# Hedgehog attention with spectral mixing: the last Z and Y copied whole and split by small transfers

## The chip, the cores and the metric

The kernel runs on one core of a Trainium2 chip. The metric is device time in microseconds for one execution. The engines are PE (TensorE, matrix products), DVE (VectorE), ACT (ScalarE), POOL (GpSimd) and SP (SyncE, which only issues transfers). PE writes its results into PSUM; DVE and ACT bring them from there to SBUF; transfers (DMA) move data between SBUF and DRAM, and between places in SBUF.

## What is computed

Linear attention with exponential features over 8 batches, 8 heads, 576 tokens and head width 64 gives x of 8 x 576 x 512. A spectral layer follows: of the Fourier transform of x along the tokens the lowest 64 modes are multiplied by complex 512 x 512 weights, one pair for each mode, and transformed back. A pointwise layer with ReLU ends it.

```python
def _moe_ref(x, w_r, w_i, w_ch):
    X = np.fft.rfft(x, axis=1)
    Y = np.zeros_like(X)
    Xr, Xi = (np.real(X[:, :n_modes]), np.imag(X[:, :n_modes]))
    Yr = np.einsum('bmd,mde->bme', Xr, w_r) - np.einsum('bmd,mde->bme', Xi, w_i)
    Yi = np.einsum('bmd,mde->bme', Xr, w_i) + np.einsum('bmd,mde->bme', Xi, w_r)
    Y[:, :n_modes] = Yr + 1j * Yi
    y = np.fft.irfft(Y, n=S, axis=1)
    u = x + y
    return (u + np.maximum(u @ w_ch, 0.0)).astype(np.float32)
```

The weights w_r and w_i are 2 x 64 x 512 x 512 numbers of 4 bytes and make up most of what is read.

## The kernel before

Everything up to the result of the last modes is the same in both kernels. In a first loop (L549) the attention is worked out in 32 pieces and x is written to `xs_all` in bf16, 5 chunks of 128 tokens for each batch (the fifth is half full). Beside it the weights stream in through POOL's queue (`weights`, L156), and `mode_mm` (L390) multiplies them as they land, in 32 steps (`groups`, L108; most of them are 8 modes for one of four groups of 128 input features). The second loop (L727 to L756) does the last ten of these steps and, between them, multiplies x by w_ch (`times_w`, result `xw`).

In the last group of features the sums are finished: `mode_sum` (L439) gives `yst`, 8 modes by 4 kinds of row, transposed on PE into `ptY` (L742) and copied to `sY` (L745). After two such steps 16 modes are complete, and `by_batch` (L691) is called with P = 0 to 3. It forms, with rows sorted by batch, Z = Y times w_ch in `psZ` (PSUM buffer T0, L699) and Y itself in `psR` (T1, L705). A batch number is j + 4 h, and in PSUM j is the block of 32 partitions and h the half of the columns. The four `copy(j)` then move block j to partitions 32 P to 32 P + 31 of `zall` and `yall`, where all modes of a batch lie one below the other: Z by ACT (L712), Y by DVE (L713). For P < 3 these copies are spread over later steps. For P = 3 the list holds five pieces: products and copy for half h = 0 and j = 0, the same for h = 1, then both halves of j = 1, 2 and 3, the last of them all on ACT.

What is left is the transform back and the sum, over 20 units (L799 to L831). A unit is two chunks of 128 tokens of one batch, or (a half unit) the fifth chunks of two batches. Batches come in pairs b and b + 4. With b = 0 to 3 a pair has four full units and one half unit: units 0 to 4, 5 to 9, 10 to 14, and 15 to 19 (in the last pair the half unit comes first). For each unit, in PE's order:

- `add_xw` (L771): an identity product brings xw into `psB`; `add_z` (L778) adds the inverse transform of Z from `zall`; ACT takes the ReLU of it to the output tile `o` (L780).
- `spec` (L787, L790): an identity product brings x into `psA`, the inverse transform of Y from `yall` is added, and DVE adds psA to o (L793). In ten "late" units (`late`, L675) the identity product is left out, and POOL adds x to o instead (L797).

`psB` and `psA` lie in PSUM buffers T2 and T3, or T0 and T1, two banks each. T0 and T1 hold psZ and psR until the last copies are done, so units 0 to 3 all use T2 and T3, and from unit 4 on even units use T2/T3 and odd ones T0/T1. Between units 0 to 3 the five pieces of `copies` are placed.

Instructions of one engine run in the order in which they are written (`manual_schedule`). SP issues the output transfers (L831), two of 256 KB for each full unit and two of 128 KB for each half unit, in its own fixed order: those of a late unit two units after it, the others at once. The output tiles `of` of a batch pair share three buffers, so pair 3 writes where pair 0 was.

Of the kernel before, what the change touches and what calls it, by code (L numbers as in the profile page):

```python
# [20 lines left out]
DMODEL = 512  # L21
# [5 lines left out]
def kernel(  # L27
# [128 lines left out]
    def weights(k):  # L156
        g, gi = groups[k]
        wt = {}
        for ri, w in ((0, moe_w_r), (1, moe_w_i)):
            t = pw.tile([128, 8, DMODEL], BF16, name=f"w{'ri'[ri]}", tag=f"w{ri}")  # L160
            if gi >= 0:
                nc.gpsimd.dma_start(  # L162
                    t, w[8 * gi:8 * gi + 8, g * 128:(g + 1) * 128, :].rearrange("m p e -> p m e"))
            else:
                for x in range(2):
                    mx = 16 * (-1 - gi) + 8 * x
                    nc.gpsimd.dma_start(
                        t[64 * x:64 * x + 64],
                        w[mx:mx + 8, g * 64:(g + 1) * 64, :].rearrange("m p e -> p m e"))
            wt[ri] = t  # L170
        W[k] = wt
# [252 lines left out]
    def mode_sum(k, psY, pb=None):  # L424
        g, gi = groups[k]
        if gi < 0:
            G = -1 - gi
            if g == 0:
                nc.vector.tensor_copy(Yacc[:, 2 * G:2 * G + 2, :], psY)
            else:  # L430
                nc.vector.tensor_tensor(
                    out=Yacc[:, 2 * G:2 * G + 2, :], in0=psY, in1=Yacc[:, 2 * G:2 * G + 2, :],
                    op=ALU.add)
        elif g < 3:
            nc.vector.tensor_tensor(  # L435
                out=Yacc[:, gi, :], in0=psY, in1=Yacc[:, gi, :], op=ALU.add)
# [254 lines left out]
    def by_batch(sY, P):  # L691
        cols = [sY[:, dc].rearrange("p g c -> p (g c)") for dc in range(4)]
        psZ = psum.tile([128, 2, DMODEL], F32, name="psZ", tag="T0")
        psR = psum.tile([128, 2, DMODEL], F32, name="psR", tag="T1")

        def mm_z(h):
            for dc in range(4):
                for j in range(4):
                    nc.tensor.matmul(psZ[32 * j:32 * j + 32, h, :], lhsT=cols[dc][:, j + 4 * h::8],  # L699
                                     rhs=wchb[:, dc, :], start=(dc == 0), stop=(dc == 3))  # L700

        def mm_r(h):
            for dc in range(4):
                for j in range(4):
                    nc.tensor.matmul(  # L705
                        psR[32 * j:32 * j + 32, h, dc * 128:(dc + 1) * 128],
                        lhsT=cols[dc][:, j + 4 * h::8], rhs=ident_b, start=True, stop=True)

        def copy(j, h=None, one=False):
            r = slice(32 * j, 32 * j + 32)  # L710
            bs, hs = (slice(j, None, 4), slice(0, 2)) if h is None else (j + 4 * h, h)
            nc.scalar.copy(zall[32 * P:32 * P + 32, bs, :], psZ[r, hs, :])  # L712
            (nc.scalar.copy if one else nc.vector.tensor_copy)(  # L713
                yall[32 * P:32 * P + 32, bs, :], psR[r, hs, :])

        if P < 3:
            for f in (mm_z, mm_r):
                for h in range(2):
                    f(h)
            copies.extend([lambda j=j: copy(j) for j in range(4)])  # L720
        else:

            copies.extend([lambda: (mm_z(0), mm_r(0), copy(0, 0)),
                           lambda: (mm_z(1), mm_r(1), copy(0, 1)),
                           lambda: copy(1), lambda: copy(2), lambda: copy(3, None, True)])

    with tc.manual_schedule():  # L727
        plan = {22: 3, 23: 3, 24: 2, 25: 2, 26: 2, 27: 1, 28: 2, 29: 1, 30: 1, 31: 0}
        while k_out < 32:
            k = k_out  # L730
            gi = groups[k][1]
            while k_in < min(k_out + NW, 32):
                weights(k_in)
                k_in += 1
            yst = mode_sum(k, mode_mm(k, "T3"), pb)
            k_out += 1
            if yst is not None:
                if ahead:
                    times_w()
                pt = psum.tile([128, 4, 128], BF16, name="ptY", tag="T3")  # L740
                for dc in range(4):
                    nc.tensor.transpose(pt[:, dc, :], yst[:, dc * 128:(dc + 1) * 128], ident_b)  # L742
                if gi % 2 == 0:
                    sY = pb.tile([128, 4, 2, 128], BF16, name="sY", tag="sY")
                nc.vector.tensor_copy(sY[:, :, gi % 2, :], pt)  # L745
                if gi % 2 == 1:
                    by_batch(sY, gi // 2)
            pieces(plan[k])
            if k <= 24 or k % 2 == 0:
                assert not copies  # L750
                for tag in ("T0", "T1"):
                    if reorder:
                        reordered(tag)
            if k == 30:
                times_w()
        assert not todo and not ahead and not reorder and len(copies) == 5  # L756

# [21 lines left out]
                             start=False, stop=True)  # L779
        nc.scalar.activation(u["o"], ps[:, 0, :] if u["half"] else ps, ACT.Relu)  # L780

    def spec(u):
        ps = psum.tile([128, 2, DMODEL], F32, name="psA", tag=u["tags"][1])
        late = u["late"]
        if not late:
            for r, x, b, c, idn, ci in parts(u):
                nc.tensor.matmul(ps[r, x, :], lhsT=idn, rhs=xs_all[:, b * NCH + c, :],  # L787
                                 start=True, stop=False)
        for r, x, b, c, idn, ci in parts(u):
            nc.tensor.matmul(ps[r, x, :], lhsT=ci, rhs=yall[:, b, :],  # L790
                             start=late, stop=True)
        o = u["o"]
        nc.vector.tensor_tensor(out=o, in0=ps[:, 0, :] if u["half"] else ps, in1=o, op=ALU.add)  # L793
        if late:
            b, c = u["bc"][0]
            i = b * NCH + c
            nc.gpsimd.tensor_tensor(out=o, in0=o, in1=xs_all[:, i:i + 2, :], op=ALU.add)  # L797

    units = []  # L799
    for b in range(4):  # L800
        of = [pw.tile([128, 4, DMODEL], F32, name="of", tag=f"w{x}") for x in range(2)]
        o4 = Yacc[:, 2 * b, :]
        us = []
        for x in range(2):
            out_v = out[b + 4 * x].rearrange("(p n) e -> p n e", n=9)
            for c in (0, 2):
                us.append(dict(bc=((b + 4 * x, c), (b + 4 * x, c + 1)), o=of[x][:, c:c + 2, :],
                               late=(x, c) in late[b], half=False,
                               dmas=[(out_v[:, 5 * jj + c:5 * jj + c + 2, :],
                                      of[x][jj::2, c:c + 2, :]) for jj in range(2)]))  # L810
        u4 = dict(bc=((b, 4), (b + 4, 4)), o=o4, late=False, half=True,
                  dmas=[(out[b + 4 * x].rearrange("(p n) e -> p n e", n=9)[:, 4, :],
                         o4[64 * x:64 * x + 64]) for x in range(2)])
        units += [u4] + us if b == 3 else us + [u4]

    with tc.manual_schedule():
        LAG = 2
        copies.pop(0)()
        for n in range(len(units) + LAG):
            if n < len(units):  # L820
                u = units[n]
                u["tags"] = ("T2", "T3") if n % 2 == 0 or n < 4 else ("T0", "T1")
                add_xw(u)
                add_z(u)
                spec(u)
                if copies:
                    copies.pop(0)()
            for lag, is_late in ((LAG, True), (0, False)):
                if 0 <= n - lag < len(units) and units[n - lag]["late"] == is_late:
                    for dst, src in units[n - lag]["dmas"]:  # L830
                        nc.sync.dma_start(dst, src)  # L831

# [29 lines left out]
```

## Time and profile before

| | us |
|---|---|
| time, median of 3 runs | 461.41 (459.97 to 462.96) |
| profiled execution, its time | 459.81 |
| profiled execution, its span | 458.0 |
| busy in the span: PE, DVE, ACT, POOL | 302.9, 299.2, 263.7, 195.2 |
| mean granted clock of PE | 0.885 |

The page gives shares over the whole span. The chain that ended last names the weights' transfers with 19% (w_i) and 7% (w_r), and the queue that carries them is busy all the time:

```profile
q0 software_dynamic: 75600, 76.49, 100.6%
q1 hardware_dynamic: 8576, 20.06, 12.6%
```

The columns are the queue, its packets, its megabytes and the time its packets took as a share of 16 engines' span. The second line is SP's queue with the inputs v and the outputs. Of the 40 slices of the span, the last four or so are the 20 units:

```profile
PE   3465687755587677646464665676678878867893
DVE  6588889867988788866656473766332274464774
ACT  4575787843676868755545453755333445663762
POOL 4956567445563346634344332533021113000593
DMA  6999999999999999999999999999999999991488
```

Each digit is one slice of 11.45 us, in tenths busy. The weights' stream ends in the slice in which DMA falls to 1; the outputs fill the last two.

### The profile page before, as it was taken

Reading aid. Unit: us, or ns where it says so; the run is one execution under the profiler, and the core shown is the slowest. Engines: PE = TensorE matmul, PEld = TensorE weight load, DVE = VectorE, ACT = ScalarE, POOL = GpSimd, SP = SyncE. Lnnn points to the kernel's source line nnn. Section 1 sums busy time; section 2 is a strip of 40 time slices with the busy share of each in tenths; the row PEclk is TensorE's granted clock in tenths of the full one; section 3 lists DMA queues with packets and bytes.
Section 4 is the critical chain, followed back from the end, with each engine's and each line's share of the span. In section 5 each row is a group of like instructions: output and inputs, shape, how many; then the busy total and the mean of one; then the engine's idle time right before and its main releaser. Section 6 shows DMA issues by size and latency. Waiting matters only on the chain.

```text
span 458.0 us, 11074 instructions
## 1 busy us (share of the span) xinstructions
PE 302.9 (66%) x4637; PEld 196.9 (43%) x4637; DVE 299.2 (65%) x418; ACT 263.7 (58%) x531; POOL 195.2 (43%) x246
## 2 busy tenths in 40 slices
PE   3465687755587677646464665676678878867893
PEld 2354465543454545534343443343344544433341
DVE  6588889867988788866656473766332274464774
ACT  4575787843676868755545453755333445663762
POOL 4956567445563346634344332533021113000593
PEclk9987999975976979997769685988999999999998
DMA  6999999999999999999999999999999999991488
GB/s 181 193 230 216 213 210 218 229 207 229 218 218 218 229 218 229 219 228 217 219 207 221 216 219 218 207 209 206 207 207 207 207 207 207 207 173 50 170 317 292
DMA packets 84385, 97.31 MB, mean 212 GB/s; under 512 B 3312, under 2 KB 77168, under 8 KB 84336
## 3 DMA queue, kind: packets, MB, share of 16 engines
q0 software_dynamic: 75600, 76.49, 100.6%
q1 hardware_dynamic: 8576, 20.06, 12.6%
q8 instruction: 36, 0.59, 0.5%
q14 instruction: 13, 0.11, 0.1%
q10 hardware_dynamic: 160, 0.07, 0.1%
HBM read 163.64 MB, written 9.44 MB: 378 GB/s over the span
## 4 chain that ended last, share of the span: by engine, by line
DMA 30%; DVE 23%; issue 21%; PE 10%; POOL 7%; ACT 7%; SPq 1%; DVEq 0%; ACTq 0%; POOLq 0%
DMA wi<-in_moe_w_i_dram 19%; DVE mkq L233 7%; DMA wr<-in_moe_w_r_dram 7%; DMA q<-in_q_dram 4%; DVE xs_all L336 4%; DVE nd L322 3%; DVE tB L315 3%; ACT AA L240 3%; POOL vaug L270 2%; ACT e L262 2%; DVE of L793 2%; PE psNB L305 2%; PE psB L771 1%; PE psB L778 1%; PE psA L790 1%
## 5 line engine op out<-in xcount | busy, mean ns | idle before, releaser
L270 POOL TENSOR_TENSOR vaug<-vn,ee 128x576 bf16<-128x576 f32 x64 | 72.7, 1156 | 59.5 <-ACT ee L255 53.6
L240 ACT ACTIVATE AA<-psT 128x1024 bf16<-128x1024 f32 x64 | 62.0, 1021 | 42.3 <-PE psT L208 41.8
L162 POOL DMA_DIRECT2D wr<-in_moe_w_r_dram x24 | 21.9, 911 | 115.9 <-PE psY L416 109.5
L262 ACT ACTIVATE e<-mkq 64x4 f32<-64x4 f32 (+1 forms) x128 | 26.3, 206 | 66.3 <-DVE mkq L233 64.0
L244 ACT ACTIVATE AA<-psk 128x1024 bf16<-128x1024 f32 x64 | 61.3, 1009 | 0.0
L416 PE MATMUL psY<-wi,XT 128*32 128x512 bf16 x192 | 24.1, 448 | 29.1 <-DMA wi<-in_moe_w_i_dram 29.1
L416 PEld LDWEIGHTS <-XT 128*32 128x32 bf16 x384 | 17.7, 167 | 55.9 <-issue 47.9
L233 DVE TENSOR_REDUCE mkq<-psk 128x8 f32<-128x1024 f32 x32 | 38.8, 1212 | 0.8 <-PE psk L199 0.7
L233 DVE TENSOR_REDUCE mkq<-psq 128x8 f32<-128x1024 f32 x32 | 38.9, 1217 | 0.3
L435 DVE TENSOR_TENSOR Yacc<-psY,Yacc 128x512 f32<-128x512 f32 x16 | 11.0, 689 | 42.6 <-PE psY L416 42.5
L797 POOL TENSOR_TENSOR of<-of,xs_all 128x1024 f32<-128x1024 f32 x10 | 21.1, 2130 | 41.5 <-DVE of L793 41.5
L661 ACT CAST xw<-psW 128x1024 bf16<-128x1024 f32 x17 | 17.2, 1012 | 36.5 <-PE psW L659 36.5
L286 PE MATMUL kvz<-vaug,AA 64*128 64x65 bf16 x1152 | 29.5, 211 | 9.7 <-POOL vaug L275 8.0
L190 DVE COPY kT<-ptr 128x640 bf16<-128x640 bf16 x32 | 15.7, 491 | 30.5 <-PE ptr L184 30.5
L416 PE MATMUL psY<-wr,XT 128*32 128x512 bf16 x192 | 24.2, 458 | 16.0 <-DMA wr<-in_moe_w_r_dram 7.3
L315 DVE TENSOR_TENSOR tB<-psNB,e 128x650 f32<-128x650 f32 x32 | 26.6, 833 | 11.4 <-PE psNB L305 10.8
L659 PE MATMUL psW<-wchb,sT 128*128 128x512 bf16 x136 | 32.2, 379 | 2.1 <-ACT xw L661 2.1
L336 DVE TENSOR_TENSOR xs_all<-nd,rden 128x640 bf16<-128x640 f32 x32 | 31.6, 988 | 1.1
L305 PEld LDWEIGHTS <-AA 128*128 128x128 bf16 x640 | 28.4, 108 | 8.9 <-issue 8.5
L286 PEld LDWEIGHTS <-AA 64*128 64x128 bf16 x1152 | 25.3, 107 | 14.5 <-issue 10.4
L208 PE MATMUL psT<-qT,w 64*128 64x512 bf16 x64 | 14.6, 446 | 23.5 <-DVE mkq L233 23.3
L322 DVE TENSOR_TENSOR nd<-psNA,tB 128x650 f32<-128x650 f32 x32 | 26.7, 835 | 4.1 <-DVE tB L315 0.5
(130 smaller groups left out, 707.3 us busy)
## 6 DMA issues: line engine op xcount, KB each, us to landing
wr<-in_moe_w_r_dram POOLq DMA_DIRECT2D x24, 1024.0 KB, 24.3
wi<-in_moe_w_i_dram POOLq DMA_DIRECT2D x24, 1024.0 KB, 28.4
wr<-in_moe_w_r_dram POOLq DMA_DIRECT2D x16, 512.0 KB, 14.9
wi<-in_moe_w_i_dram POOLq DMA_DIRECT2D x16, 512.0 KB, 18.6
out_dram<-of SPq DMA_DIRECT2D x32, 256.0 KB, 2.4
vn<-in_v_dram SPq DMA_DIRECT2D x24, 288.0 KB, 5.7
q<-in_q_dram POOLq DMA_DIRECT2D x12, 288.0 KB, 19.5
k<-in_k_dram POOLq DMA_DIRECT2D x12, 288.0 KB, 19.3
```

The source lines that it names most:

```text
L233: nc.vector.tensor_reduce(out=o, in_=i, axis=AX.X, op=ALU.max, apply_absolute_value=True)
L240: nc.scalar.activation(AA[:, 0, ab, 0:1024].rearrange("f (x j p) -> f j x p", j=2, p=64), st["psT"].rearrange("f j (x p) -> f j x p", p=64 ...
L244: nc.scalar.activation(AA[:, 1, ab, 0:1024].rearrange("p (c j f) -> p j c f", c=4, j=2), st["psk"], ACT.Exp, scale=sc)
L262: nc.scalar.activation(e2[64 * jj:64 * jj + 64, hh, 0:NCH - jj], mkq[64 * hh:64 * hh + 64, 1, 5 * jj:5 + 4 * jj], ACT.Exp, scale=2.0)
L270: nc.gpsimd.tensor_tensor(out=vaug[:, ab, :, 0:64], in0=st["v"], in1=ee[:, ab, :].unsqueeze(2).to_broadcast([128, 9, D_]), op=ALU.mult,)
L286: nc.tensor.matmul(kvz[:, hh, ab * 65:(ab + 1) * 65], lhsT=AA[r, 1, ab, 128 * j:128 * j + 128], rhs=vaug[r, ab, j, :], start=(j == 0), sto ...
L305: nc.tensor.matmul(p[:, hh, 65 * c:65 * c + 65], lhsT=AA[:, 0, ab, x:x + 128], rhs=kvzF[:, hh, ab * 65:(ab + 1) * 65], start=True, stop=True,)
L315: nc.vector.tensor_tensor(out=tB, in0=st["psNB"], in1=e2.unsqueeze(3).to_broadcast([128, 2, NCH, 65]), op=ALU.mult,)
L322: nc.vector.tensor_tensor(out=nd, in0=st["psNA"], in1=st["tB"], op=ALU.add)
L336: nc.vector.tensor_tensor(out=xo, in0=nd[:, :, :, 0:64], in1=rden.to_broadcast([128, 2, NCH, 64]), op=ALU.mult,)
L416: nc.tensor.matmul(psY[32 * j:32 * j + 32, :], lhsT=XT[:, c0:c0 + 32, m], rhs=wt[ri][:, 2 * j + par, :], start=(par == 0 and ri == 0), sto ...
L659: nc.tensor.matmul(ps[:, x, :], lhsT=sT[:, x, dc, :], rhs=wchb[:, dc, :], start=(dc == 0), stop=(dc == 3))
```

## The change

In `by_batch` the last call (P = 3) no longer leaves its copies to later. It makes the products of half h = 0, copies block j = 0 of that half, does the same for h = 1, and then copies psZ and psR whole, each in one instruction, to two new SBUF tiles `stz` and `sty` (ACT and DVE). Six transfers of 64 KB from SBUF to SBUF bring blocks j = 1, 2 and 3 of both to their places in `zall` and `yall`: the pair for j = 1 (batches 1 and 5) through SP's queue, those for j = 2 and 3 through POOL's.

Unit 0's two identity products are moved ahead: `add_xw(u0)` into T2 before the products of the last step of modes, and `add_x(u0)` into T3 behind the last transposes, whose target `ptY` is put into T1 in that step. `spec` is split into `add_x` and `spec` for this. All units now alternate between T2/T3 and T0/T1 from the start.

For batch pairs 1 and 2 the two full units of a batch are sent together, as two transfers of 512 KB with 8 KB in each row, not four of 256 KB with 4 KB in each row. They are placed in SP's order one unit after the second one (three, if that is a late one). Late units of pairs 0 and 3 are sent three units behind and not two. In SP's order the last four units, 16 to 19, are sent as 18, 16, 19, 17; before they were sent as 16, 18, 17, 19.

```diff
@@ by_batch
-        def copy(j, h=None, one=False):
+        rows = slice(32 * P, 32 * P + 32)
+
+        def copy(j):
             r = slice(32 * j, 32 * j + 32)
-            bs, hs = (slice(j, None, 4), slice(0, 2)) if h is None else (j + 4 * h, h)
-            nc.scalar.copy(zall[32 * P:32 * P + 32, bs, :], psZ[r, hs, :])
-            (nc.scalar.copy if one else nc.vector.tensor_copy)(
-                yall[32 * P:32 * P + 32, bs, :], psR[r, hs, :])
+            nc.scalar.copy(zall[rows, j::4, :], psZ[r])
+            nc.vector.tensor_copy(yall[rows, j::4, :], psR[r])
...
-        else:
-
-            copies.extend([lambda: (mm_z(0), mm_r(0), copy(0, 0)),
-                           lambda: (mm_z(1), mm_r(1), copy(0, 1)),
-                           lambda: copy(1), lambda: copy(2), lambda: copy(3, None, True)])
+            return
+        stz, sty = [pb.tile([128, 2, DMODEL], BF16, name=nm, bufs=1) for nm in ("stz", "sty")]
+        for h in range(2):
+            mm_z(h)
+            mm_r(h)
+            nc.scalar.copy(zall[rows, 4 * h, :], psZ[0:32, h, :])
+            nc.vector.tensor_copy(yall[rows, 4 * h, :], psR[0:32, h, :])
+        nc.scalar.copy(stz, psZ)
+        nc.vector.tensor_copy(sty, psR)
+        for j in range(1, 4):
+            for dst, src in ((zall, stz), (yall, sty)):
+                (nc.sync if j == 1 else nc.gpsimd).dma_start(
+                    dst[rows, j::4, :], src[32 * j:32 * j + 32])
...
+    def add_x(u):
+        u["psA"] = ps = psum.tile([128, 2, DMODEL], F32, name="psA", tag=u["tags"][1])
+        if not u["late"]:
+            for r, x, b, c, idn, ci in parts(u):
+                nc.tensor.matmul(ps[r, x, :], lhsT=idn, rhs=xs_all[:, b * NCH + c, :],
+                                 start=True, stop=False)
...
+    u0 = dict(bc=((0, 0), (0, 1)), half=False, late=False, tags=("T2", "T3"))
...
+            if k == 31:
+                add_xw(u0)
             yst = mode_sum(k, mode_mm(k, "T3"), pb)
...
-                pt = psum.tile([128, 4, 128], BF16, name="ptY", tag="T3")
+                pt = psum.tile([128, 4, 128], BF16, name="ptY", tag="T3" if k < 31 else "T1")
...
+                if k == 31:
+                    add_x(u0)
...
+        whole = b in (1, 2)
...
+                c0 = 0 if whole else c
+                is_late = (x, c) in late[b]
                 us.append(dict(bc=((b + 4 * x, c), (b + 4 * x, c + 1)), o=of[x][:, c:c + 2, :],
-                               late=(x, c) in late[b], half=False,
-                               dmas=[(out_v[:, 5 * jj + c:5 * jj + c + 2, :],
-                                      of[x][jj::2, c:c + 2, :]) for jj in range(2)]))
+                               late=is_late, half=False,
+                               lag=3 if is_late else 1 if whole else 0,
+                               dmas=[(out_v[:, 5 * jj + c0:5 * jj + c + 2, :],
+                                      of[x][jj::2, c0:c + 2, :]) for jj in range(2)]
+                               if c == 2 or not whole else []))
...
     with tc.manual_schedule():
-        LAG = 2
-        copies.pop(0)()
-        for n in range(len(units) + LAG):
+        for n, u in enumerate(units):
+            u["tags"] = ("T2", "T3") if n % 2 == 0 else ("T0", "T1")
+        for n in range(len(units) + 3):
             if n < len(units):
                 u = units[n]
-                u["tags"] = ("T2", "T3") if n % 2 == 0 or n < 4 else ("T0", "T1")
-                add_xw(u)
+                if n:
+                    add_xw(u)
                 add_z(u)
+                if n:
+                    add_x(u)
                 spec(u)
-                if copies:
-                    copies.pop(0)()
-            for lag, is_late in ((LAG, True), (0, False)):
-                if 0 <= n - lag < len(units) and units[n - lag]["late"] == is_late:
+            for lag in (3, 1, 0):
+                if 0 <= n - lag < len(units) and units[n - lag]["lag"] == lag:
                     for dst, src in units[n - lag]["dmas"]:
                         nc.sync.dma_start(dst, src)
```

More of the change, by code (lines that the diff above doesn't have):

```diff
@@ L720, in by_batch @@
             copies.extend([lambda j=j: copy(j) for j in range(4)])
-        else:
-            copies.extend([lambda: (mm_z(0), mm_r(0), copy(0, 0)),
-                           lambda: (mm_z(1), mm_r(1), copy(0, 1)),
-                           lambda: copy(1), lambda: copy(2), lambda: copy(3, None, True)])
[L727 to L739, printed above, removed]
-                pt = psum.tile([128, 4, 128], BF16, name="ptY", tag="T3")
[L741 to L756, printed above, removed]
+            return
[11 more added lines that the diff above has]
+                    dst[rows, j::4, :], src[32 * j:32 * j + 32])
     def parts(u):
@@ L780, in add_z @@
         nc.scalar.activation(u["o"], ps[:, 0, :] if u["half"] else ps, ACT.Relu)
[L782 to L785, printed above, removed]
+    def add_x(u):
+        u["psA"] = ps = psum.tile([128, 2, DMODEL], F32, name="psA", tag=u["tags"][1])
+        if not u["late"]:
             for r, x, b, c, idn, ci in parts(u):
@@ L788, in spec @@
                                  start=True, stop=False)
+    def spec(u):
+        ps, late, o = u["psA"], u["late"], u["o"]
         for r, x, b, c, idn, ci in parts(u):
@@ L791, in spec @@
                              start=late, stop=True)
-        o = u["o"]
         nc.vector.tensor_tensor(out=o, in0=ps[:, 0, :] if u["half"] else ps, in1=o, op=ALU.add)
@@ L797, in spec @@
             nc.gpsimd.tensor_tensor(out=o, in0=o, in1=xs_all[:, i:i + 2, :], op=ALU.add)
+    u0 = dict(bc=((0, 0), (0, 1)), half=False, late=False, tags=("T2", "T3"))
+    with tc.manual_schedule():
+        plan = {22: 3, 23: 3, 24: 2, 25: 2, 26: 2, 27: 1, 28: 2, 29: 1, 30: 1, 31: 0}
+        while k_out < 32:
+            k = k_out
+            gi = groups[k][1]
+            while k_in < min(k_out + NW, 32):
+                weights(k_in)
+                k_in += 1
+            if k == 31:
+                add_xw(u0)
+            yst = mode_sum(k, mode_mm(k, "T3"), pb)
+            k_out += 1
+            if yst is not None:
+                if ahead:
+                    times_w()
+                pt = psum.tile([128, 4, 128], BF16, name="ptY", tag="T3" if k < 31 else "T1")
+                for dc in range(4):
+                    nc.tensor.transpose(pt[:, dc, :], yst[:, dc * 128:(dc + 1) * 128], ident_b)
+                if k == 31:
+                    add_x(u0)
+                if gi % 2 == 0:
+                    sY = pb.tile([128, 4, 2, 128], BF16, name="sY", tag="sY")
+                nc.vector.tensor_copy(sY[:, :, gi % 2, :], pt)
+                if gi % 2 == 1:
+                    by_batch(sY, gi // 2)
+            pieces(plan[k])
+            if k <= 24 or k % 2 == 0:
+                assert not copies
+                for tag in ("T0", "T1"):
+                    if reorder:
+                        reordered(tag)
+            if k == 30:
+                times_w()
+        assert not todo and not ahead and not reorder and not copies
     units = []
@@ L806 @@
             for c in (0, 2):
+                c0 = 0 if whole else c
+                is_late = (x, c) in late[b]
                 us.append(dict(bc=((b + 4 * x, c), (b + 4 * x, c + 1)), o=of[x][:, c:c + 2, :],
-                               late=(x, c) in late[b], half=False,
-                               dmas=[(out_v[:, 5 * jj + c:5 * jj + c + 2, :],
-                                      of[x][jj::2, c:c + 2, :]) for jj in range(2)]))
-        u4 = dict(bc=((b, 4), (b + 4, 4)), o=o4, late=False, half=True,
+                               late=is_late, half=False,
[3 more added lines that the diff above has]
+                               if c == 2 or not whole else []))
+        u4 = dict(bc=((b, 4), (b + 4, 4)), o=o4, late=False, half=True, lag=0,
                   dmas=[(out[b + 4 * x].rearrange("(p n) e -> p n e", n=9)[:, 4, :],
@@ L814 @@
         units += [u4] + us if b == 3 else us + [u4]
+    units[0].update(psA=u0["psA"], psB=u0["psB"])
     with tc.manual_schedule():
-        LAG = 2
-        copies.pop(0)()
-        for n in range(len(units) + LAG):
+        for n, u in enumerate(units):
+            u["tags"] = ("T2", "T3") if n % 2 == 0 else ("T0", "T1")
+        for n in range(len(units) + 3):
             if n < len(units):
                 u = units[n]
-                u["tags"] = ("T2", "T3") if n % 2 == 0 or n < 4 else ("T0", "T1")
-                add_xw(u)
+                if n:
+                    add_xw(u)
                 add_z(u)
+                if n:
+                    add_x(u)
                 spec(u)
-                if copies:
-                    copies.pop(0)()
-            for lag, is_late in ((LAG, True), (0, False)):
-                if 0 <= n - lag < len(units) and units[n - lag]["late"] == is_late:
+            for lag in (3, 1, 0):
+                if 0 <= n - lag < len(units) and units[n - lag]["lag"] == lag:
                     for dst, src in units[n - lag]["dmas"]:
```

## The prediction

> **What bounds the kernel now.** I read the slices of the page first, then the stretches of the end, the timeline of that end, and the rows of single instructions. The order of both programs shows the same instructions with the same waits on all engines up to the last mode's products; all that differs lies behind about 412 us. Up to there the kernel runs at the pace of the weight stream, whose last half is awaited at 413.06:
>
> ```profile
> 388.44 24.57 DMA wi<-in_moe_w_i_dram
> 413.01 0.04 issue
> 413.06 0.93 PE psY L416 x10
> ```
>
> So only the last 45 us can move. Cut into stretches (start:end, length, busy time and count of PE, weight loads, DVE, ACT, POOL, clock, DMA share, GB/s):
>
> ```profile
> 416.00:424.00 8.00, 7.51 (x86) 3.64 (x79) 4.35 (x5) 4.90 (x6) 0.00 (x0) 1.00 0.17 67
> 424.00:429.00 5.00, 2.74 (x15) 0.87 (x13) 4.36 (x4) 4.84 (x6) 2.58 (x2) 1.00 0.26 105
> 429.00:450.60 21.60, 21.12 (x106) 8.89 (x104) 16.05 (x15) 13.87 (x16) 17.15 (x9) 1.00 0.81 289
> 450.60:458.00 7.40, 0.00 (x0) 0.00 (x0) 1.22 (x1) 0.14 (x1) 1.38 (x1) 0.79 0.74 292
> ```
>
> From 429 to 450.6 PE is full (21.12 of 21.60); the clock is 1.00, so PE's pace cannot be improved there. The hole is 424 to 429: PE works 2.74 of 5.00 while ACT (4.84) and DVE (4.36) are full. The timeline says with what:
>
> ```profile
> 423.49 0.59 PE L790 MATMUL psA<-yall,CI 128*128 128x512 bf16 x2 [0.24 <-DVE of L793]
> 424.34 1.00 ACT L712 CAST zall<-psZ 32x1024 bf16<-32x1024 f32 x1
> 424.37 0.59 PE L771 MATMUL psB<-xw,ident_p 128*128 128x512 bf16 x2 [0.28 <-ACT of L780]
> 425.98 1.22 DVE L713 CAST yall<-psR 32x1024 bf16<-32x1024 f32 x1
> 426.00 0.59 PE L790 MATMUL psA<-yall,CI 128*128 128x512 bf16 x2 [0.61 <-DVE of L793]
> 427.39 1.00 ACT L713 CAST yall<-psR 32x1024 bf16<-32x1024 f32 x1
> 428.51 0.41 PE L787 MATMUL psA<-xs_all,ident_b 128*64 128x512 bf16 x2 [1.37 <-DVE of L793]
> ```
>
> The copies of psZ and psR (L712, L713) stand between the Relus and the adds, and hold T0 and T1, so units 0 to 4 share T2/T3 and each waits for its predecessor's DVE add. The end:
>
> ```profile
> 447.76 4.22 POOL L797 TENSOR_TENSOR of<-of,xs_all 128x1024 f32<-128x1024 f32 x2 [1.05 <-DVE of L793]
> 449.92 4.99 SPq L831 DMA_DIRECT2D out_dram<-of  x8
> 450.78 1.22 DVE L793 TENSOR_TENSOR of<-psA,of 128x1024 f32<-128x1024 f32 x1 [0.45 <-ACT of L780]
> ```
>
> SP issues the last eight transfers back to back, 4.99/8 = 0.62 us each, from 449.92, when POOL is done with unit 16; the span ends 3.1 us behind the last of them (458.0 - 454.9).
>
> **The change part by part.** I walk the units through by fixed rows: 0.215 us per product of 512 columns (the L771 pairs 0.43 apart), Relu 1.02, add 1.23 (half unit 0.60 and 0.69), late add on POOL 2.11 (4.22/2), an SP issue 0.62. The same walk over the kernel before starts unit 5 at 428.82 (trace: 429.06) and its last issue at 453.70 (trace: 454.3), so 0.2 to 0.6 short; I use differences of two walks only.
>
> *Products ahead.* add_xw(u0) must wait for the last copy of xw (ACT, 411.04 to 412.05) and then takes 0.43; the wr products behind it, at 410.93 before, come to about 412.5 to 412.75. The wi weights arrive at 413.01: hidden, with 0.26 to spare; if they landed at once it would cost up to that. add_x(u0) runs while DVE copies sY (0.42). Gain: 0.86 of unit 0.
>
> *The two halves of Z and R together.* The first psZ copy runs 416.81 to 417.38, and the second half's products wait for it by the order's semaphores (417.43, a wait of 0.43 since PE is free at 417.00); they end at 418.74 (1.07 + 0.24). Unit 0's remaining products: 419.60.
>
> *Whole copies.* ACT: second zall piece 418.57 to 419.14, stz to 420.17. DVE: second yall piece from 418.9, sty to 420.85. The prices are those of the rows nearest in shape: xw L661, 128x1024, 1.01 on ACT, and yall 32x1024, 1.22 on DVE. Taken off: three ACT copies of 1.00, two DVE copies of 1.22, and yall's one on ACT. Behind stz are queued all Relus: unit 0's moves from 418.07 to 420.19, and its add from 419.12 to 421.24, two microseconds later than before (sty holds back nothing more: the first add waits for its Relu until 421.2). That is the price of the change. Bounds for the pair: 0.57/0.68 (the 32x512 rows) gives 0.45 more gain, 2.0/2.5 costs 1.0.
>
> *T0 and T1 free.* Unit 1 waits for stz (420.22), ends at 421.94; unit 2 at 423.23, unit 3 at 424.53, unit 4 at 425.75 (0.38 of it waiting for unit 2's add). The waits of the copied timeline lines are gone. Unit 5 starts at 425.75 against 428.82: 3.07 earlier. From there to unit 19 both walks take the same, PE being full in both.
>
> *Six transfers.* SP's pair for batches 1 and 5 is issued at 420.2 and 420.9, and unit 0's output behind them is not ready before 422.5: nothing lost on SP. They are needed at 426.0 and 426.6. The trace has no SBUF-to-SBUF transfer; its SP rows land in 2.2 to 4.0 us with no weights in flight (vn in the full queue 5.7), so 422.6 to 426.6: hidden. No landing, however fast, gains anything. POOL issues the other four from 420.2; small issues of its queue are these:
>
> ```profile
> L143 POOL DMA_DIRECT2D q<-in_q_dram x12: 752/756/767, 46.7 to 238.3; - x12
> L162 POOL DMA_DIRECT2D wr<-in_moe_w_r_dram x24: 873/926/946, 115.0 to 387.6; - x24
> ```
>
> Four at 0.75 to 0.95 end at 423.2 to 424.3 (the second waits for sty); POOL's first late add is wanted at 425.3. Covered by 1 us. Batches 2 and 6 are wanted at 433.0, batches 3 and 7 at 439.6; even a landing of 5 to 6 us (the 144 KB q and k rows) is early.
>
> The Trainium skill ("SBUF — State Buffer", two separate sides) says that a POOL-issued DMA cannot write its descriptors while DVE runs in a two-port mode. The row speaks against that here: the issues took 0.70 to 0.95 throughout attention, where DVE was 5 to 9 tenths busy, and DVE reads PSUM in all of this stretch. What it would do here is rival 2.
>
> *Longer rows, other order.* Eight issues fewer, 8 x 0.6 = 5 us of SP, none of them among the last eight, in front of which SP was idle (447.15 to 449.92 holds four issues of 0.6). Price nothing. x0 of batch 1 leaves only with POOL's unit 5 (431.7), which lets DMA idle; what follows, 7.2 MB at the 404 GB/s of the fullest slices, is done by 449.5, when the last issues are still going out. The lag of 3 changes SP's order at the end to units 18, 16, 19, 17.
>
> *The sum.* PE, DVE and POOL run 3.07 earlier from unit 5 on. The last eight issues now begin with unit 18's add, not unit 16's POOL add, 0.41 later in relation: -3.07 + 0.41 = -2.66. Eight issues and the landing behind them are as before. The profiled execution took 459.81 (span 458.0), so 457.15; it lay 1.6 under the median of the runs, 461.41, which gives 458.7.
>
> **Rivals.**
> 1. *The end is not held by SP's pace.* If the last eight go out as they become ready, the end follows unit 19's add and four issues: about -3.5, median 457.9. For it: DMA share falls to 0.74 at the end. Against: eight issues without a gap at 0.62. 0.15.
> 2. *Less is won.* If each POOL issue also sits out one DVE add (0.87 + 1.23 = 2.1 us), four end at 428.7, 3.4 late; POOL's idle time takes up 1.9 of that, and 1.5 reaches the end: -1.15, median 460.3. For it: DVE adds without a gap from 421.2 on. Against: the 0.70 to 0.95 beside a busy DVE. 0.06. Copies at 2.0/2.5 give -1.6, median 459.8: 0.07.
> 3. *Slower: POOL becomes the bound.* It has 10 x 2.11 = 21.1 us of late adds between 425.3 and 448.4, idle under 2 us in all. Each microsecond more per issue delays them by four once that and the 1 us of cover are gone: nothing is won from 2.4 us per issue on, and at 3.5 the kernel is 4.4 us slower, 465.8. For it: this is the first use of POOL's queue from SBUF. Against: no row over 0.95. The same end comes from SP's pair landing later than 8.4 us. 0.09.
> 4. *The early units do not change*, since the second half's products and stz move unit 0 back by as much as T0/T1 give: 0 to -0.5, median 461.2. Against: the walk's 3 us, three waits of PE that have no cause left. 0.04.
>
> **How the numbers follow.** The forecast, 458.7, has 0.59. A median of this kernel's runs is told from no change at about 1%, 4.6 us; the runs shown spread over 3.0, so a median by some 0.8 either way. Faster by over 1% (under 456.8): a tenth of the forecast and nearly half of rival 1, 0.13. Slower by over 1%: most of rival 3, 0.07. Within 1%: 0.80. The range from 456.4 (rival 1 with its scatter) to 461.4 (rivals 2 and 4) leaves out a bit of both ends and rival 3.
>
> **What would show it.** In the profile after: Relu of unit 0 near 420.2 past the weights' 413.0 (7.2 us behind), unit 5's first product 12.7 us behind it; no PE wait for the pieces of zall and yall; POOL's four issues under 1 us; PE, DVE and POOL ending 3 us earlier relative to the weights' arrival; eight last issues 0.62 apart. Wrong is the forecast if PE waits at unit 5 or 10 for a transfer, if POOL's late adds trail DVE by more than 3 us, or if the end behind the last issue is not 3.1.

## The result

| | before | changed |
|---|---|---|
| median, us | 461.32 (459.45 to 464.0, 14 runs) | 457.53 (456.67 to 461.03, 14 runs) |
| ratio to before, 95% interval | | 0.9932 (0.9907 to 0.9956) |
| profiled execution, us | 459.81 | 456.96 |
| its span | 458.0 | 455.2 |
| start of the last sum of the modes (yst) | 414.01 | 414.03 |
| from there to the end of the span | 43.99 | 41.17 |

The changed kernel is faster by 0.7%, 2.0 to 4.3 us of 461; the forecast was 2.7. Measured once more (e11 below), it was faster by 0.4%, 1.1 to 2.7 us. Both are within the 1% that was called "no change". The two profiled executions start the last sum of the modes, `yst`, at the same time, so their spans differ by what lies behind it: 43.99 - 41.17 = 2.82 us. In the following, "+" times count from the start of yst in the same trace.

The stretches of the end, changed kernel, columns as before:

```profile
416.00:424.00 8.00, 7.08 (x86) 4.03 (x79) 5.03 (x5) 5.08 (x6) 2.17 (x4) 1.00 0.22 53
424.00:429.00 5.00, 4.91 (x27) 1.93 (x26) 4.00 (x4) 3.38 (x5) 3.60 (x2) 1.00 0.63 233
429.00:447.40 18.40, 17.97 (x91) 7.46 (x89) 14.40 (x14) 12.07 (x14) 16.02 (x9) 1.00 0.89 336
447.40:455.20 7.80, 0.00 (x1) 0.00 (x0) 1.23 (x1) 0.20 (x1) 1.44 (x1) 0.84 0.67 269
```

The hole between 424 and 429 is closed: PE is busy 4.91 of 5.00 where it was 2.74, with the same clock of 1.00. From there PE is full as before, and its last pair of products starts 3.16 us earlier (+32.78 for +35.94). The start of the units:

```profile
419.18 1.01 ACT L731 CAST stz<-psZ 128x1024 bf16<-128x1024 f32 x1
419.53 1.23 DVE L732 CAST sty<-psR 128x1024 bf16<-128x1024 f32 x1
420.09 1.03 ACT L760 ACTIVATE of<-psB 128x1024 f32<-128x1024 f32 x1
420.24 0.59 PE L751 MATMUL psB<-xw,ident_p 128*128 128x512 bf16 x2 [0.48 <-ACT stz L731]
420.86 0.56 POOL L735 DMA_DIRECT2D zall<-stz  x1 [31.28 <-issue]
425.40 4.22 POOL L778 TENSOR_TENSOR of<-of,xs_all 128x1024 f32<-128x1024 f32 x2 [2.36 <-DVE of L774]
```

Unit 0's Relu waits for the whole copy and comes 2 us later than before; unit 1 waits 0.48 for T0, and that is PE's last wait for a copy. Behind yst no wait of PE for a transfer is in the trace. POOL is done with its four issues at 423.04 and waits 2.36 us for its first late add. The end:

```profile
443.71 8.47 SPq L856 DMA_DIRECT2D out_dram<-of  x10
444.62 4.22 POOL L778 TENSOR_TENSOR of<-of,xs_all 128x1024 f32<-128x1024 f32 x2 [1.04 <-DVE of L774]
447.21 1.11 SPq L856 DMA_DIRECT2D out_dram<-of  x2
447.63 1.23 DVE L774 TENSOR_TENSOR of<-psA,of 128x1024 f32<-128x1024 f32 x1 [0.46 <-ACT of L760]
```

The group of ten is batch pair 2's last two transfers and the last eight, which start with unit 18's at 447.21, though POOL was done with unit 16 at 446.73 (444.62 + 2.11).

### The profile page after: what moved, and what is told of

It is laid out like the page before. It is cut to its first block, busy times and chain, and to the rows that moved or that the text cites. A ratio compares the mean times of both kernels' runs of the same rounds, so it can differ in the third digit from the quotient of the medians.

```text
span 455.2 us, 11075 instructions
## 1 busy us (share of the span) xinstructions
PE 305.3 (67%) x4637; PEld 199.0 (44%) x4637; DVE 295.8 (65%) x417; ACT 261.2 (57%) x528; POOL 196.9 (43%) x250
## 4 chain that ended last, share of the span: by engine, by line
DMA 30%; PE 24%; DVE 24%; ACT 8%; issue 6%; POOL 5%; SPq 1%; DVEq 0%; ACTq 0%; POOLq 0%
DMA wi<-in_moe_w_i_dram 14%; DMA k<-in_k_dram 6%; DVE mkq L233 6%; PE psW L659 6%; DMA wr<-in_moe_w_r_dram 5%; DMA q<-in_q_dram 5%; DVE xs_all L336 3%; DVE nd L322 3%; DVE tB L315 3%; ACT AA L240 2%; PE psY L416 2%; POOL vaug L270 2%; PE psZ L699 2%; DVE yall L714 2%; ACT e L262 2%
## 5 line engine op out<-in xcount | busy, mean ns | idle before, releaser
L661 ACT CAST xw<-psW 128x1024 bf16<-128x1024 f32 x17 | 17.2, 1012 | 36.4 <-PE psW L659 30.5
L336 DVE TENSOR_TENSOR xs_all<-nd,rden 128x640 bf16<-128x640 f32 x32 | 29.5, 921 | 1.1
L184 PE MATMUL ptr<-ident_b,k 128*128 128x128 bf16 x160 | 17.6, 254 | 14.8 <-DVE qT L190 13.0
```

The costliest lines, as they stand in the source:

```text
L336: nc.vector.tensor_tensor(out=xo, in0=nd[:, :, :, 0:64], in1=rden.to_broadcast([128, 2, NCH, 64]), op=ALU.mult,)
```

## The experiments

The stretch in front of yst is the same program in all kernels but for what is told below, and it scatters: in the fourteen profiled executions yst starts between 413.5 and 419.5. An effect below 1 us is therefore read from the time behind yst, which repeats within 0.3 us (the changed kernel, profiled twice: 41.17 and 41.11), and the ratios are given beside it. The spans are given to 0.1 us, so each of these times can be off by 0.05.

| kernel | ratio to before (interval) | yst to end of span |
|---|---|---|
| before | 1 | 43.99 |
| changed; once more | 0.9932 (0.9907-0.9956); 0.9958 (0.9941-0.9976) | 41.17; 41.11 |
| e1, output transfers as before | 0.9945 (0.9925-0.9965) | 40.71 |
| e2, output transfers alone | 1.0012 (0.9991-1.0032) | 44.45 |
| e3, first products not ahead | 0.9923 (0.9901-0.9946) | 41.13 |
| e4, copies by engines | 1.0005 (0.9984-1.0026) | 43.41 |
| e5, 16 more POOL issues (2 runs) | 1.0052 (1.0032-1.0072) | 44.98 |
| e6, all six on SP | 0.9979 (0.9960-0.9998) | 40.88 |
| e7, order at the end (2 runs) | 0.9940 (0.9918-0.9961) | 40.69 |
| e8, no late unit in pair 3 | 0.9946 (0.9926-0.9966) | 40.21 |
| e9, add_xw behind the mode products | 0.9930 (0.9908-0.9953) | 41.15 |
| e10, best parts together | 0.9923 (0.9901-0.9946) | 40.66 |
| e12, add_xw ahead alone | 1.0018 (0.9994-1.0042) | 44.05 |

### Longer rows: taken out (e1) and alone (e2)

```diff
-        whole = b in (1, 2)
+        whole = False
-                               lag=3 if is_late else 1 if whole else 0,
+                               lag=2 if is_late else 1 if whole else 0,
```

> The changed kernel with the output transfers as before (256 KB each, late units two units behind, order 16, 18, 17, 19 at the end); copies, transfers of Z and Y and first products stay changed. Theory (the gain is the early units', the longer rows give nothing and their order costs about 0.4 us at the end): the last eight issues start with unit 16's POOL add, near 446.7 where the changed kernel starts them at 447.2; time 0.3 to 0.5 us below the changed kernel, 3.1 to 3.5 below before. Rival (longer rows relieve SP or the DMA engines): 1 us or more slower than the changed kernel, and SP's issues of units 5 to 13 trail POOL's adds.

e2 is the kernel before with the changed kernel's `whole`, `lag` and `dmas` and its order of issues.

> The kernel before with only the changed output transfers (longer rows for pairs 1 and 2, three units' lag, order 18, 16, 19, 17). Theory: nothing is won, the last eight start with unit 18's add instead of unit 16's POOL add, 0.3 to 0.5 us later: same as before to 0.5 slower. Rival (longer rows carry the gain): 1.5 to 3 us faster than before.

Without the changed transfers the end comes 0.46 earlier, with them alone 0.46 later. Both are the theory's sizes, and both are one thing, the order: e1 starts its last eight with unit 16, as soon as POOL has finished it. SP's line of e1:

```profile
450.55 4.99 SPq L856 DMA_DIRECT2D out_dram<-of  x8
```

That is +32.76, and unit 16's add on POOL ended at +32.73; the changed kernel starts them at +33.18. The ratios (0.9945 for e1, 0.9932 for the changed kernel) cannot tell 0.5 us. The rival, that longer rows carry the gain, falls with e2: no ratio below 0.9991.

### First products not ahead (e3), and ahead alone (e12)

```diff
-            if k == 31:
-                add_xw(u0)
...
-                if k == 31:
-                    add_x(u0)
...
-                if n:
-                    add_xw(u)
+                add_xw(u)
```

> The changed kernel with unit 0's two identity products back in their place between the others. Theory: PE waits 0.5 us for the whole copy of psZ at unit 1 in the changed kernel, so of the 0.86 us that the products take only 0.2 to 0.4 is seen; unit 1 starts 0.2 to 0.4 later, time 0.2 to 0.4 above the changed kernel. Rival (the prediction's line, 0.86 of gain): unit 1 and all behind it 0.8 to 0.9 later.

In the program built from this, PE's order has unit 0's `add_xw` right behind the last step's mode products and only `add_x` among the units, so e3 undoes half of what it was to undo, and moves the other half. The end is at +41.13: nothing is lost by add_x. PE waits for stz in unit 1 either way. The timeline of e3:

```profile
418.61 0.59 PE L766 MATMUL psA<-xs_all,ident_p 128*128 128x512 bf16 x2
419.05 0.59 PE L772 MATMUL psA<-yall,CI 128*128 128x512 bf16 x2
419.53 1.03 ACT L760 ACTIVATE of<-psB 128x1024 f32<-128x1024 f32 x1
419.69 0.59 PE L751 MATMUL psB<-xw,ident_p 128*128 128x512 bf16 x2
```

Here add_x (L766) stands where PE would be idle; the Relu and unit 1 (L751) come at +6.06 and +6.22, as in the changed kernel (+6.06, +6.21). Of PE's wait some 0.2 us is left (spec's two products start at 419.05, 0.43 later PE is free, and unit 1 starts at 419.69). With add_xw (0.43) among the units too, unit 1 would thus start an estimated 0.2 later, the low end of what was expected; no run shows it.

e12 is the kernel before with two products added in front of the last step's mode products, and unit 0's own left out:

```diff
+            if k == 31:
+                psB0 = psum.tile([128, 2, DMODEL], F32, name="psB", tag="T2")
+                for x in range(2):
+                    nc.tensor.matmul(psB0[:, x, :], lhsT=ident_p, rhs=xw0[:, x, :],
+                                     start=True, stop=False)
             yst = mode_sum(k, mode_mm(k, "T3"), pb)
```

> The kernel before with add_xw of unit 0 alone put ahead of the last step's mode products, all else as before. Theory: 0.43 is won behind yst (end at +43.5 to +43.6, before +43.99), and yst comes 2.80 behind the last psW product, which costs up to 1.6 where the weights are early: 0 to 1.2 slower than before. Rival (the prediction's line, hidden by the weights): 0.4 faster than before and yst not later relative to the weights' end.

```profile
409.87 1.89 PE L659 MATMUL psW<-wchb,sT 128*128 128x512 bf16 x8
412.85 0.59 PE L738 MATMUL psB<-xw,ident_p 128*128 128x512 bf16 x2 [1.10 <-ACT xw L661]
413.38 0.47 PE L416 MATMUL psY<-wr,XT 128*32 128x512 bf16 x4
413.69 0.47 PE L416 MATMUL psY<-wi,XT 128*32 128x512 bf16 x4
```

The wait is as expected: PE waits 1.10 us for ACT's copy of psW, and yst comes 2.89 behind the last psW product. In this execution it costs nothing, though: by the trace the last w_i transfer landed at 413.65, so the w_i products at 413.69 could not have come sooner. The gain is not as expected: the end is at +44.05 and not +43.5. Unit 0's Relu starts at +4.06 with and without it, since add_z waits for the first zall copy, and the 0.43 only fills that wait. The ratio, 1.0018 (0.9994 to 1.0042), allows for anything from 0.3 us faster to 1.9 slower.

### Copies by the engines (e4)

```diff
-        nc.scalar.copy(stz, psZ)
-        nc.vector.tensor_copy(sty, psR)
         for j in range(1, 4):
-            for dst, src in ((zall, stz), (yall, sty)):
-                (nc.sync if j == 1 else nc.gpsimd).dma_start(
-                    dst[rows, j::4, :], src[32 * j:32 * j + 32])
+            copy(j)
```

> The changed kernel without whole copies and transfers: the three remaining blocks are copied by ACT and DVE, one after the other, before unit 0 (three of 1.00 and three of 1.22 us in place of one each). Theory (what pays is that one whole copy takes the place of three): unit 0's Relu comes 2.0 us later, its add 2.1, and all behind them; time 1.8 to 2.2 above the changed kernel, about 0.6 to 1.2 below before. Rival (what pays is only that the copies stand ahead of the units and T0 and T1 come free): as fast as the changed kernel within 0.5.

The Relu waits 2.0 us longer, as the timeline of ACT in e4 shows:

```profile
420.84 3.04 ACT L713 CAST zall<-psZ 32x1024 bf16<-32x1024 f32 x3
423.90 2.11 ACT L755 ACTIVATE of<-psB 128x1024 f32<-128x1024 f32 x2
```

That is +8.21 (changed kernel +6.06), and the end comes at +43.41, 2.24 later, close to the 1.8 to 2.2 of the theory and far from the rival's 0.5. So one copy in place of three is worth about 2.2 of the 2.8 us. The other 0.6 is what the rest of the change gives with the order's loss of 0.46 taken off: mainly, it is argued, T0 and T1 free early; no run takes that part out alone. A copy of 32 partitions takes ACT as long as one of 128 (3.04/3 = 1.01; stz 1.01); the transfers put the parts in the places to which otherwise only narrow copies bring them.

### POOL's and SP's queues (e5, e6)

```diff
+        dum = pb.tile([128, 4, 128], BF16, name="dum", bufs=1)
+        for i in range(16):
+            r = slice(32 * (i % 4), 32 * (i % 4) + 32)
+            nc.gpsimd.dma_start(dum[r, i // 4, :], (stz, sty)[i % 2][r, 0, 0:128])
```

> The changed kernel with 16 more small transfers on POOL's queue behind its four (32 x 128 numbers each, from stz and sty to an unused tile). Measured from the start of the last sum of the modes (yst), the changed kernel's span ends at +41.17. Theory (POOL's queue is covered, and has 2.4 us to spare between its late adds): at 0.55 us per issue POOL's first late add moves from +11.4 to about +20 - of these 8.8 us, 2.4 at the start and 2.4 between the adds are absorbed - and the end comes 2.4 to 3.4 us later, at +43.6 to +44.6. Rival (POOL's adds are far from the path): the end stays within 0.5 of +41.17. Rival (each issue delays what follows in full): +46 or more.

```profile
432.18 0.50 POOL L740 DMA_DIRECT2D dum<-sty  x1
432.70 20.91 POOL L782 TENSOR_TENSOR of<-of,xs_all 128x1024 f32<-128x1024 f32 x10
```

POOL's ten adds now follow each other without a gap, 20.91 us, and its last ends at +37.79 in place of +34.81. Of the 7.9 us that the 16 issues take (0.49 each), 2.4 are absorbed in front of the first add (+16.88; +20 was a slip in adding up) and 2.5 between the adds; 3.0 reach POOL's end and 3.8 the span's, a little more than the theory's most (3.4). So POOL can decide the end; in the changed kernel some 4.9 us more of work in front of its first late add would be absorbed before its own end moves.

```diff
-                (nc.sync if j == 1 else nc.gpsimd).dma_start(
+                nc.sync.dma_start(
```

> The changed kernel with all six transfers of Z and Y on SP's queue. Theory (neither queue is on the path there): SP is busy with them to about 4 us behind the first, unit 0's output goes out 1.8 us later, nothing else moves: end at +41.17 within 0.2 from the start of yst. Rival (SP's issues hold the whole output back): the end comes 1.5 to 2.5 us later.

PE, DVE and POOL end at the changed kernel's + times within 0.02, SP's last issue too (+38.14 for +38.15), so behind yst it is all the same which queue takes the six. The span ends 0.29 earlier, a little outside what was expected, but the last transfer lands at +39.99 in both traces: the difference lies behind all transfers, and the part behind the last issue varied from 2.7 to 3.4 us over all traces. The ratio, 0.9979 (0.9960 to 0.9998), is above the changed kernel's first interval. Nothing behind yst is slower, so that difference would lie in front of yst (416.42 here); one execution was profiled, and these runs do not show why.

### The order at the end and the late units (e7, e8)

```diff
-                               lag=3 if is_late else 1 if whole else 0,
+                               lag=(2 if b == 3 else 3) if is_late else 1 if whole else 0,
```

> The changed kernel with SP's order at the end as before, 16, 18, 17, 19 and not 18, 16, 19, 17; longer rows stay. Theory: the last eight issues start with unit 16's POOL add, 0.45 us earlier, and the span ends at +40.6 to +40.8 from the start of yst (changed kernel: +41.17). Rival (the DMA engines are full there with the longer rows of the pair before): no change within 0.1.

The end is at +40.69: as expected, 0.48 gained, with the longer rows in place.

```diff
-            3: ((0, 0), (0, 2))}
+            3: ()}
```

> The changed kernel with no late units in the last pair: PE adds x in units 16 and 17 too, POOL does eight adds and not ten. Theory (the end is set by when the first of the last eight issues can start and then by 0.62 us for each): PE ends 0.9 later, but unit 16 is ready two microseconds earlier, and the end is bound by unit 19's add and two issues: +39.9 to +40.3 from the start of yst, 1 us gained. Rival (PE sets the end): +41.9 to +42.1, 0.8 slower.

The end is at +40.21, as expected. PE's last pair starts at +33.64, 0.86 later, and yet the whole ends 0.96 earlier: unit 16 is ready at +30.5 (changed kernel: +32.7), and the last eight begin at +31.0. Unit 19's add ends at +35.69, and its two issues start at +35.71, as the theory said; they land 2.7 to 2.8 us behind their issue, where the changed kernel's last ones take 2.4 (see the last section). PE, busiest in this stretch, does not set the end. Its profiled execution is also the one with the latest yst (419.49); the last psW product ended late in it (416.70), which says nothing on the edit.

### add_xw behind the mode products (e9), and the best parts (e10), beside the changed kernel (e11)

```diff
-            if k == 31:
-                add_xw(u0)
-            yst = mode_sum(k, mode_mm(k, "T3"), pb)
+            psY = mode_mm(k, "T3")
+            if k == 31:
+                add_xw(u0)
+            yst = mode_sum(k, psY, pb)
```

> The changed kernel with add_xw of unit 0 put behind the products of the last step of modes in PE's order (it runs while DVE forms yst), not ahead of them. In all seven kernels with it ahead, yst starts 2.80 us behind the last psW product: add_xw waits for ACT's copy of psW (1.0), then the mode products follow. Theory (this wait is on the path when the weights are there by then, which was so in five of seven profiled executions): yst starts 1.1 to 1.3 behind the last psW product where the weights are early, and 1.0 to 1.5 behind the weights' end where they are late; the span behind yst stays +41.17; time 0.5 to 1.5 us below the changed kernel. Rival (the weights come last anyway): no change within 0.3.

> The changed kernel as it is, once more, beside the two kernels above on the same chip. All theories: ratio to before 0.991 to 0.995, yst 2.80 behind the last psW product, span end at +41.0 to +41.3.

First e1, which has add_xw ahead as the changed kernel does, then e9:

```profile
413.10 1.89 PE L659 MATMUL psW<-wchb,sT 128*128 128x512 bf16 x8
416.09 0.59 PE L751 MATMUL psB<-xw,ident_p 128*128 128x512 bf16 x2 [1.10 <-ACT xw L661]
416.61 0.47 PE L416 MATMUL psY<-wr,XT 128*32 128x512 bf16 x4
417.79 0.69 DVE L439 TENSOR_TENSOR yst<-psY,Yacc 128x512 bf16<-128x512 f32 x1 [3.68 <-PE psY L416]
```

```profile
412.77 1.89 PE L659 MATMUL psW<-wchb,sT 128*128 128x512 bf16 x8
414.59 0.47 PE L416 MATMUL psY<-wr,XT 128*32 128x512 bf16 x4
415.30 0.47 PE L416 MATMUL psY<-wi,XT 128*32 128x512 bf16 x4 [0.24 <-DMA wi<-in_moe_w_i_dram]
416.13 0.39 PE L751 MATMUL psB<-xw,ident_p 128*128 128x512 bf16 x1
```

In e1 the mode products start 1.62 us behind the last psW product's end (413.10 + 1.89 = 414.99), though DMA's share had fallen to 0.01 by 414.8 and no wait for weights is left. In e9 they follow at once, wait 0.24 for the weights, and yst starts at 416.25, 1.59 behind psW's end where e1 has 2.80, and 1.00 behind the landing of the last w_i transfer (415.25), as expected. Medians on the same chip: 457.22 for e9 (6 runs), 458.68 for e11 (12 runs), 1.5 apart; the intervals of the ratios overlap (0.9908-0.9953 and 0.9941-0.9976), so the time leans to the theory and does not prove it. e11's ratio, 0.9958, lies just above what was expected, and its trace repeats the first.

e10 adds `3: ()` and e1's edit to e9.

> add_xw of unit 0 behind the mode products, no late units in the last pair, output transfers of 256 KB in the order of before; copies and six transfers as changed. Theory: the parts add up: +39.8 to +40.3 from the start of yst (changed kernel +41.17), and yst up to 1.6 us nearer to the last psW product: 1.5 to 2.5 us below the changed kernel, 4.5 to 5.5 below before, ratio 0.988 to 0.991. Rival (the DMA engines set the end once the first of the last eight comes earlier): +40.5 to +41.2 and a ratio of 0.992 or more.

Its end is at +40.66, as the rival said, and so is its ratio, 0.9923, though the interval reaches into the theory's range. The reason is another than the rival's:

```profile
443.53 1.19 SPq L857 DMA_DIRECT2D out_dram<-of  x2
444.82 1.19 SPq L857 DMA_DIRECT2D out_dram<-Yacc  x2
446.10 1.18 SPq L857 DMA_DIRECT2D out_dram<-of  x2
```

Unit 16 is ready at 444.06 (its add, 442.83 + 1.23), and SP comes to it at 446.10: it is still issuing earlier units. In e8, with longer rows, SP begins the last eight 0.45 behind unit 16's add. So the longer rows are worth about 0.4 at the end once unit 16 is early (40.66 against 40.21), and cost nothing but their order. The combination of e9, e8 and the longer rows was not run; none of the kernels tried is faster than the changed one beyond the intervals.

## Why the prediction was right

**The sum.** Forecast -2.66 in the profiled execution; behind yst it is -2.82. Unit 5 was to start 3.07 earlier; it does so 3.16 earlier (425.92 with yst at 414.03, before 429.06 with 414.01). The loss of 0.41 from SP's order is there: 0.46 by e1 and e2, 0.48 by e7. The times of the walk: Relu of unit 0 at 420.19 (420.09), unit 1 at 420.22 (420.24), the last eight, 2.66 before 449.92, at 447.26 (447.21). The agreement within 0.2 us is that of the profiled executions; the median, forecast at 458.7, came to 457.53 the first time and 458.68 the second, and such medians scatter by more than that agreement.

**Whole copies, T0 and T1.** Right in mechanism and size. e4 shows the main share: one copy in place of three gives about 2.2. The order takes 0.46 back, so 1.0 is left for T0 and T1 free early; that share is found by subtraction and not shown by a run of its own.

**Six transfers.** Hidden, as forecast. They landed in 1.9 to 2.3 us, at the low end of the bounds 2.2 to 4.0 or below; POOL's issues took 0.55 to 0.56, below the rows 0.75 to 0.95 used, so the cover was 2.36 us and not 1. The Trainium skill ("DMA: Bandwidth & Descriptors", Anatomy of one DMA) gives, for transfers that POOL issues, 2.0 us fixed plus the bytes at 436 GB/s; for 64 KB that is an estimated 2.15, and POOL's four in the changed kernel agree with 1.93 to 2.26. The rule of the Trainium skill on POOL's descriptors and DVE ("SBUF — State Buffer", two separate sides) is not tested, since no trace shows the mode in which DVE ran: beside adds of DVE that read PSUM, POOL issued one transfer every 0.50 us in e5.

**Longer rows, other order.** "Price nothing" holds for the changed kernel (e1, e2 and e7 account for all of it by the order). It would not hold with an earlier unit 16 (e10).

**Products ahead.** This step failed, twice, without moving the forecast much. The prediction put "Gain: 0.86 of unit 0" and, for the products in front of the mode products, "hidden, with 0.26 to spare". The gain is next to nothing: for add_x nothing, since PE would wait for stz in any case (e3); for add_xw nothing in the kernel before, where PE would wait for zall (e12), and an estimated 0.2 in the changed one. And the cover was that of one execution, in which the weights came last.

Two times of each trace tell what it costs: P, when the last psW product ends, and L, when the last w_i transfer lands. In the five traces without add_xw ahead, yst starts at the later of P + 1.16 and L + 1.00; in the nine with it, at the later of P + 2.79 and L + 1.00. All fourteen agree within 0.02 us. So in five of the nine executions (e1, e4, e6, e7, e8) it cost 1.5 to 1.6 us, and in four (the changed kernel twice, e5, e12) nothing, since the weights landed 1.8 to 1.9 behind P: an estimated 0.9 on average. That the weights landed late in both of the first two profiles (413.01 with P at 411.00, 413.02 with P at 411.24) is luck, and let the sum come out. The walk behind yst could not show the cost, since it lies in front of yst. The ratios lean the same way and do not prove it: of the kernels with whole copies, the three without add_xw ahead (e3, e9, e10) have 0.9923 to 0.9930, those with it and no added issues 0.9932 to 0.9979.

**The rivals.** 1 (SP's pace does not hold the end) did not come in the changed kernel, whose last eight issues follow each other without a gap, 0.62 apart. It is half right as to the start: e7 and e8 show that the end follows the first of the last eight, and e8 that behind it SP's pace need not be what holds the end (last section). 2 and 4 fall with the times above. 3 did not come, but was the right place to look: e5 shows POOL deciding the end once it has enough to do. Its slack was larger than the 1 us of cover and under 2 us of idle time that were forecast: 2.4 and 2.5.

## What to carry to other kernels

Where the front of a kernel scatters by more than the change is worth, measure from an event that both kernels share, in the trace. A step that is moved ahead to fill a wait brings its own waits with it; ask what it costs in the executions in which the awaited thing is already there, not only in the one profiled. A copy out of PSUM took as long here for 32 partitions as for 128 (ACT 1.00 and 1.01 us, DVE 1.22 and 1.23), so one whole copy and a few small transfers can replace several narrow copies, if something is left to do while the transfers land.

## What had not been expected

The time to the last sum of the modes varies by 6 us between executions of nearly the same program (413.5 to 419.5), twice the whole gain, while the 41 to 45 us behind it repeat to 0.3.

It had not been expected either that the DMA engines can be what holds the end. In twelve of the fourteen traces SP's last eight transfers of 256 KB are issued 0.62 us apart and land 0.64 apart, 2.3 to 2.5 us behind their issue, and the pace of SP and that of the engines cannot be told apart. In e5 and e8, when the eight begin, transfers of 512 KB are still under way for another 3.0 us (0.7 in the changed kernel). There the second issue takes 1.2 us and the third starts 1.3 behind it, as SP's line of e8 shows (the second and the third):

```profile
451.22 1.89 SPq L856 DMA_DIRECT2D out_dram<-of  x2
```

Landing takes 2.7 to 3.7 us, and yet the eight land 0.64 apart as elsewhere. So the pace there is not set by SP's issues; 256 KB in 0.64 us is 410 GB/s, and in e8 the DMA engines show a share of 1.00 to 1.03 from 453.5 to 457.5, with 399 to 412 GB/s.
